# Stage changes of a fused attention and two-layer kernel: operand pool at the bottom, fourth output operand split at once, last product's operands formed in place

## The chip, the cores and the metric

The kernel runs on 1 core of one Trainium2 chip. The metric is the device time of one execution in microseconds (us), as the median of several executions. A profiled execution has a time of its own and a span, which runs from its first to its last instruction. Engines are called PE (matmul), PEld (weight load of the PE), DVE (VectorE), ACT (ScalarE), POOL (GpSimd) and SP (SyncE, whose queue SPq issues the transfers here). L612 means line 612 of the kernel before.

## What is computed

The reference, cut to what matters (all float32; 3072 tokens, width 512):

```
x   = chunked attention with memory keys (4 batches, 8 heads, 768 positions)   # 3072 x 512
h   = x @ w_in;   g = h * tanh(softplus(h));   y = g @ w_out                   # 512 -> 2048 -> 512
yn  = y / sqrt(mean(y*y) + 1e-6) * rms_g
out = (silu(yn @ w_gate) * (yn @ w_val)) @ w_out2                              # 512 -> 1536 -> 512
```

## The kernel before

**Stages.** The core does, one after the other with some overlap: attention (transposes and small matmuls); the first product (w_in) in groups; the output product (w_out) in 48 steps; the gate and value product in groups; and the last product (w_out2) in 12 units. Every float32 operand is split in two float32r parts, a high part written by ACT (L145) and a low part written by DVE (L146), and every product is three matmuls: high by high, high by low, low by high.

**Seven products.** The first, the gate and the last product use a scheme with seven block products instead of eight. An operand block matrix b11, b21, b12, b22 gives seven operands, numbered 1 to 7, some of them sums of blocks. `sum_pieces` forms them: operand 1 is b11; then b11 becomes b12 - b11, a first temporary is b22 - b11, a second is the first minus b21, and b12 becomes b22 - b12; operands 6, 5, 4, 2, 7, 3 are split from the first temporary, b11, the second temporary, b21, b12, b22. `group` multiplies them in the order 1, 6, 5, 4, 2, 7, 3 into four banks X, Y, Z, V: product 2 adds to X (1), 7 to Y (6), 3 to Z (5). Between them ACT copies X to s1 (L622) and Z to z5 (L628), and DVE forms u2 (L625), u3 (L636), and at the end the output blocks (L639, L641), POOL one more (L640).

**Pools in SBUF.** On the left side, above the pools that live through the kernel, lie three pools of the first product in this order from the bottom: `cp` (temporaries, 6 x 1536 bytes a partition, 9216), `gp` (results g on their way out to DRAM, 5 x 3072, 15360) and `tp` (operands, 8 x 6144, 49152). Before the output product they are closed and the same bytes are given, from the bottom, to `gl` (one tile of 4096 bytes), `c` (2 x 2048) and `t` (8 operand tiles of 8192, called T). A late tile waits for the old tiles whose bytes it covers, each until its last reader is done; for a g tile the last reader is its store to DRAM (L110). `gl` and `gr` hold one v tile each; the groups of the gate product take them in turn, and `v_temp` takes them for the two temporaries of `sum_pieces`.

**Output product.** `Feed` loads the g tile of a step from DRAM (L742), applies the activation (ACT L753), and splits it. The first three steps' operands go into borrowed tiles (named s, v, w), the fourth goes into the first T tile, by way of the only sm tile; its split is asked for in `feed.next(1)`, after the first step's matmuls and after that step's share of weight conversion (L194 to L208, then ACT L145 and POOL L146 into w; 16 of them for w_out). A step is 24 matmuls (L725 to L727).

**Last product.** `group3` runs one unit: seven products of 18 matmuls each (six weight tiles, f = 0 to 5, three matmuls each, L854 to L856). `preparing(n)` forms the operands of unit n while the work before it runs, one piece at each step of `group`: those of unit 0 during the last group of the gate product, those of unit n + 1 during unit n. Even units load into raw, raw, sm and s tiles, odd ones into the bytes of weight slot 2 (L835), which the last group of the gate product uses until its last matmul. The sixth weight tile, ("o2", 5), goes in one transfer of 1792 KB into slot 3 (L1176), free when the last group but one is done. A weight tile holds the seven products' parts in the order 1, 2, 4, 3, 5, 6, 7, each 256 KB.

**Order.** The order of the instructions on each engine is fixed when the program is built, by a planner that runs the program on a model of the engines' times and takes what is ready, the earlier in the program first. The engines then run their lists in order. So PE's list mixes products of neighbouring groups where the planner saw a wait.

Of the kernel before, what the change touches and what calls it, by code (L numbers as in the profile page):

```python
# [8 lines left out]
F32 = mybir.dt.float32  # L9
# [4 lines left out]
ALU = mybir.AluOpType  # L14
# [15 lines left out]
def tile_kernel(  # L30
# [15 lines left out]
    nc = tc.nc  # L46
# [23 lines left out]
    wd = {("i", i): nc.dram_tensor(f"wi{i}", (128, SLOT), F32R, kind="Internal").ap()  # L70
          for i in range(F1 // 2)}
# [11 lines left out]
    rawp = ctx.enter_context(tc.tile_pool(name="rawp", bufs=2))  # L83
    cap = ctx.enter_context(tc.tile_pool(name="cap", bufs=3))
    mid_stack = ExitStack()
    cp = mid_stack.enter_context(tc.tile_pool(name="cp", bufs=6))
    gp = mid_stack.enter_context(tc.tile_pool(name="gp", bufs=5))
    tp = mid_stack.enter_context(tc.tile_pool(name="tp", bufs=8))
    late_pools = {}
    psp = ctx.enter_context(tc.tile_pool(name="psp", bufs=1, space=bass.MemoryType.PSUM))  # L90
    bk = [psp.tile([128, 512], F32, name=f"bk{c}") for c in range(6)]
# [11 lines left out]
    def store_later(dst, src):  # L103
        late.append((tick[0] + 2, dst, src))
# [8 lines left out]
    def w_slot(u):  # L113
        pool = w1p if u < NW1 else w2p[0]
        return pool.tile([128, SLOT], F32R, tag=f"w{u}", name="w")
# [3 lines left out]
    def as7(s):  # L119
        return s.rearrange("p (a l f) -> p a l f", a=7, l=2)  # L120

    def w_load(key, u):
        s = w_slot(u)
        nc.sync.dma_start(out=s.bitcast(F32), in_=wd[key].bitcast(F32))
        wtab[key] = as7(s)

    def w_store(key, half):
# [16 lines left out]
    def split(src, hi, lo, eng=None, keep=lambda ins: ins):  # L144
        keep(nc.scalar.copy(hi, src))  # L145
        keep((eng or nc.vector).tensor_tensor(lo, src, hi.bitcast(F32), op=ALU.subtract))  # L146
# [399 lines left out]
    def s_new():  # L546
        return late_pools["s"].tile([128, 2, N2], F32, tag="s", name="s")
# [4 lines left out]
    def c_new():  # L552
        return late_pools["c"].tile([128, N2], F32, tag="c", name="c")
# [4 lines left out]
    def t_pieces(j, x0, x1, new, temp_new, dram, tab):  # L558

        return sum_pieces(j, x0[:, 0:2, :], x0[:, 2:4, :], x1[:, 0:2, :], x1[:, 2:4, :],  # L560
                          new, temp_new, dram, tab)

    def sum_pieces(j, b11, b21, b12, b22, new, temp_new, dram, tab):
        cols = b11.shape[2]
        size = b11.shape[1] * cols
        temp = {}

        def as_block(x):
            return x[:, 0:size].rearrange("p (a n) -> p a n", n=cols)

        def one(p, src):
            t = new()
            if isinstance(t, tuple):
                split(src, *t)
                for l in range(2):
                    store_later(dram[:, p - 1, l].bitcast(F32), t[l].bitcast(F32))
                return
            v = t.rearrange("p l a n -> p l (a n)")[:, :, 0:size]
            v = v.rearrange("p l (a n) -> p l a n", n=cols)
            split(src, v[:, 0], v[:, 1])  # L580
            if dram is not None:
                store_later(dram[:, p - 1].bitcast(F32), t.bitcast(F32))
            tab[j, p] = v

        def sums():
            for p in (2, 4):
                temp[p] = as_block(temp_new(p).rearrange("p a n -> p (a n)"))
            nc.vector.tensor_tensor(b11, b12, b11, op=ALU.subtract)
            nc.vector.tensor_tensor(temp[2], b22, b11, op=ALU.subtract)
            nc.vector.tensor_tensor(temp[4], temp[2], b21, op=ALU.subtract)  # L590
            nc.vector.tensor_tensor(b12, b22, b12, op=ALU.subtract)

        early = [lambda: one(1, b11), sums]
        rest = [lambda: one(6, temp[2]), lambda: one(5, b11), lambda: one(4, temp[4]),
                lambda: one(2, b21), lambda: one(7, b12), lambda: one(3, b22)]
        return early, rest

    def t_load(j, dram, tab):
        for p in ORDER:
            t = t_new2()  # L600
            nc.sync.dma_start(out=t.bitcast(F32), in_=dram[:, p - 1].bitcast(F32))
            tab[j, p] = t
# [10 lines left out]
            nc.tensor.matmul(ps, whi, xl, start=False, stop=False, **more)  # L613
            nc.tensor.matmul(ps, wlo, xh, start=False, stop=kk == 1, **more)  # L614

    def group(mul, banks, n_, c12, c21, c22, temps):

        X, Y, Z, V = banks
        x, y, z, vv = (b_[:, 0:n_] for b_ in banks)
        s1, u2, z5 = temps()  # L620
        mul(1, X, True)
        nc.scalar.copy(s1, x)  # L622
        yield
        mul(6, Y, True)
        nc.vector.tensor_tensor(u2, y, s1, op=ALU.add)  # L625
        yield
        mul(5, Z, True)
        nc.scalar.copy(z5, z)  # L628
        yield
        mul(4, V, True)  # L630
        yield
        mul(2, X, False)
        yield
        mul(7, Y, False)
        u3 = s1
        nc.vector.tensor_tensor(u3, y, s1, op=ALU.add)  # L636
        yield
        mul(3, Z, False)
        nc.vector.tensor_tensor(c12, z, u2, op=ALU.add)  # L639
        nc.gpsimd.tensor_tensor(c22, u3, z5, op=ALU.add)  # L640
        nc.vector.scalar_tensor_tensor(  # L641
            c21, vv, -1.0, u3, op0=ALU.mult, op1=ALU.add
        )
        yield
# [25 lines left out]
    def run(parts, between):  # L670
        while parts:
            for part in list(parts):
                if next(part, "end") == "end":
                    parts.remove(part)
                else:
                    between()
# [3 lines left out]
    def group_banks(of):  # L680
        g = n_group[0]
        n_group[0] += 1
        return [bk[(4 * g + of - 4 + i) % of] for i in range(4)]
# [45 lines left out]
    class Feed:  # L729
# [34 lines left out]
        def next(self, s):  # L764
            self.load(s + 3)
            self.split(s + 3)
            self.load(s + 5)
            return self.out.pop(0)
# [52 lines left out]
    hraw, ttab_h = {}, {}  # L821
# [17 lines left out]
        hraw[n] = parts  # L839

    def h_pieces(n):
        return sum_pieces(n, *hraw.pop(n), t_new2, v_temp, None, ttab_h)

    def group3(n, j, r, between):
        o = s_new()
        o = [o[:, a, :] for a in range(2)]

        def mul(p, bank_, first):
            t = ttab_h[n, p]
            ps = bank_[:, 0:256]  # L850
            more = dict(skip_group_check=not first)
            for f in range(HG):
                w = wtab["o2", f][:, W_AT[p]]
                nc.tensor.matmul(ps, t[:, 0, f], w[:, 0], start=first and f == 0, stop=False, **more)  # L854
                nc.tensor.matmul(ps, t[:, 0, f], w[:, 1], start=False, stop=False, **more)  # L855
                nc.tensor.matmul(ps, t[:, 1, f], w[:, 0], start=False, stop=f == HG - 1, **more)  # L856

        banks = group_banks(8)
        c11 = banks[0][:, 0:256]
        c12, c21, c22 = o[1][:, 0:256], o[0][:, 256:512], o[1][:, 256:512]  # L860
        run([group(mul, banks, 256, c12, c21, c22, lambda: (c_new()[:, 0:256], c12, c22))], between)
        nc.scalar.copy(o[0][:, 0:256], c11)
        for a in range(2):
            row = (2 * j + a) * N2 + 128 * r
            store_later(out[row:row + 128, :], o[a])
# [100 lines left out]
    def reload(pos, seq):  # L966
        if pos < 3:
            w_load(("i", seq[5 + pos]), W_SLOT[seq[5 + pos]])
# [16 lines left out]
    at = {u: 4 * n + 4 for n, u in enumerate(units)}  # L985
# [28 lines left out]
    def late_pool(name, bufs, side="left"):  # L1014
        return ctx.enter_context(tc.tile_pool(name=name, bufs=bufs, side=side, reuse_waits="tile"))
# [5 lines left out]
    for pos, i in enumerate(down[:-1]):  # L1021
        group1(3, i, bt)
        if 1 <= pos <= 3:
            back, u = ((1, 4), (2, 0), (0, 1))[pos - 1]
            w_load(("i", back), u)
# [6 lines left out]
    feed = Feed(steps, g_src, ACTF.Mish)  # L1032
# [15 lines left out]
    late_pools["gl"] = late_pool("gl", 1)  # L1048
    late_pools["c"] = late_pool("c", 2)
    late_pools["t"] = late_pool("t", 8)  # L1050
    pend = []
    sq_new = lambda: [c_new() for _ in range(2)]
    for s, (m, i) in enumerate(steps):
        t = feed.next(s)
# [18 lines left out]
        if m == NB2 - 1 and i in (1, 3, 5, 6):  # L1073
            row_slots.clear()
            f, u = {1: (2, 5), 3: (3, 6), 5: (4, 3), 6: (5, 2)}[i]
# [84 lines left out]
    for jn, j in enumerate(jback):  # L1160
        last = jn == NPAIR2 - 1
        if jn:
            t_load(j, nt_d[j], ttab_n)
            run([group2(j, HG), group2(j, HG + 1)], bt)
            if last:
                w_load(("o2", 1), 1)
                w_load(("o2", 2), 4)
        for f in range(HG + 2 if jn else HG, F2):
            run([group2(j, f)], preparing(0, bt) if last and f == F2 - 1 else bt)
            if last and f == HG + 2:  # L1170
                w_load(("o2", 3), 5)
            elif last and f == HG + 3:
                h_load(0, *units[0])
                w_load(("o2", 4), 6)
            elif last and f == HG + 4:
                w_load(("o2", 5), 3)  # L1176
    h_load(1, *units[1])
    for n, (j, r) in enumerate(units):
        if 0 < n < len(units) - 1:
# [34 lines left out]
```

## Time and profile before

| what | value |
|---|---|
| median of 3 runs | 1191.08 us (1189.69 to 1196.43) |
| the profiled execution's own time | 1190.69 us |
| its span | 1188.9 us |
| PE busy | 1153.8 us, 97% of the span |
| DVE, ACT, POOL busy | 817.5, 621.5, 215.1 us |
| mean granted PE clock | 0.990 |

A busy share near 100% says that PE sets the pace. Time can then be won in PE's few idle stretches and where its granted clock is below 1.00.

### The profile page before, as it was taken

How to read it: one execution, taken by the hardware profiler on the slowest of the kernel's cores; microseconds unless marked ns; L12 is line 12 of the kernel's file. 1: busy time of each engine (PE TensorE's matmuls, PEld its weight loads, DVE VectorE, ACT ScalarE, POOL GpSimd, SP SyncE). 2: the span in 40 equal slices, each digit the busy share in tenths (PEclk: the TensorE clock that was granted, in tenths of full speed). 3: DMA queues.
4: the chain of work that ended last, by engine and by line, in shares of the span. 5: the costliest groups of instructions: out<-in, count | busy, mean ns of one | idle time of the engine just before them, and what ended most of it. 6: DMA issues, size and time to landing. Idle time of an engine off the chain costs nothing.

```text
span 1188.9 us, 22951 instructions
## 1 busy us (share of the span) xinstructions
PE 1153.8 (97%) x9052; PEld 1008.5 (85%) x9052; DVE 817.5 (69%) x1212; ACT 621.5 (52%) x996; POOL 215.1 (18%) x185
## 2 busy tenths in 40 slices
PE   6899899999999899999999999999999999999998
PEld 4789899999999688888878878878888888999998
DVE  4655898854755856675775675976886746887773
ACT  5566566543545866667665443553454423444442
POOL 2010222310132411030131121322221211000000
PEclk8899989999999999999999999999999999999999
DMA  9889869899488764595589388899889878654420
GB/s 188 172 230 217 209 239 264 231 293 300 148 304 289 246 204 129 187 362 163 195 329 393 144 343 333 321 416 391 319 312 377 315 264 293 195 173 142 142 90 36
DMA packets 219132, 294.20 MB, mean 247 GB/s; under 512 B 104208, under 2 KB 168720, under 8 KB 210064
## 3 DMA queue, kind: packets, MB, share of 16 engines
q1 hardware_dynamic: 219024, 292.73, 74.1%
q8 instruction: 71, 1.16, 0.4%
q14 instruction: 37, 0.30, 0.1%
HBM read 181.80 MB, written 110.89 MB: 246 GB/s over the span
## 4 chain that ended last, share of the span: by engine, by line
PE 74%; DMA 8%; DVE 7%; ACT 5%; issue 3%; POOL 2%; SPq 0%; ACTq 0%; POOLq 0%; DVEq 0%
PE bk L612 13%; PE bk L614 12%; PE bk L613 12%; DMA s<-g_scratch 4%; PE bk L856 4%; PE bk L854 4%; PE bk L855 4%; PE bk L726 3%; PE bk L727 3%; PE bk L725 3%; PE bkp L612 2%; PE bkp L614 2%; PE bkp L613 2%; PE bkp L434 2%; PE bkp L483 1%
## 5 line engine op out<-in xcount | busy, mean ns | idle before, releaser
L612 PE MATMUL bk<-T,w 128*128 128x384 f32 (+1 forms) x860 | 317.3, 372 | 5.5 <-ACT g L662 4.1
L613 PE MATMUL bk<-T,w 128*128 128x384 f32 (+1 forms) x860 | 312.5, 363 | 0.0
L614 PE MATMUL bk<-T,w 128*128 128x384 f32 (+1 forms) x860 | 311.6, 364 | 0.0
L612 PEld LDWEIGHTS bk<-T,w 128*128 128x128 f32 x860 | 162.7, 190 | 26.7 <-ACT g L662 4.3
L613 PEld LDWEIGHTS bk<-T,w 128*128 128x128 f32 x860 | 162.5, 189 | 17.3 <-issue 0.2
L614 PEld LDWEIGHTS bk<-T,w 128*128 128x128 f32 x860 | 162.3, 189 | 16.8
L854 PE MATMUL bk<-w,T 128*128 128x256 f32 x396 | 112.3, 284 | 2.9 <-ACT T L145 1.8
L725 PE MATMUL bk<-T,w 128*128 128x512 f32 x276 | 109.1, 396 | 2.9 <-ACT T L145 2.9
L856 PE MATMUL bk<-w,T 128*128 128x256 f32 x396 | 111.4, 282 | 0.2 <-DVE T L146 0.2
L855 PE MATMUL bk<-w,T 128*128 128x256 f32 x396 | 111.4, 281 | 0.0
L726 PE MATMUL bk<-T,w 128*128 128x512 f32 x276 | 109.4, 396 | 0.3 <-DVE T L146 0.3
L727 PE MATMUL bk<-T,w 128*128 128x512 f32 x276 | 108.6, 393 | 0.0
L640 POOL TENSOR_TENSOR v<-c,v 128x512 f32<-128x512 f32 x36 | 51.6, 1436 | 222.3 <-DVE c L636 164.8
L636 DVE TENSOR_TENSOR c<-bk,c 128x512 f32<-128x512 f32 (+2 forms) x72 | 43.1, 599 | 63.4 <-PE bk L614 51.7
L622 ACT COPY c<-bk 128x512 f32<-128x512 f32 (+2 forms) x72 | 37.0, 516 | 83.9 <-PE bk L614 33.3
L146 DVE TENSOR_TENSOR T<-s,T 128x1024 fp32r<-128x1024 f32 (+1 forms) x50 | 61.3, 1235 | 26.0 <-ACT T L145 25.5
L854 PEld LDWEIGHTS bk<-w,T 128*128 128x128 f32 x396 | 75.2, 190 | 4.2 <-ACT T L145 2.9
L855 PEld LDWEIGHTS bk<-w,T 128*128 128x128 f32 x396 | 75.5, 191 | 0.1
L856 PEld LDWEIGHTS bk<-w,T 128*128 128x128 f32 x396 | 75.0, 190 | 0.4 <-DVE T L146 0.4
L753 ACT ACTIVATE s<-s 128x1024 f32<-128x1024 f32 x44 | 46.7, 1061 | 38.6 <-DMA s<-g_scratch 36.6
L725 PEld LDWEIGHTS bk<-T,w 128*128 128x128 f32 x276 | 51.8, 188 | 15.4 <-ACT T L145 3.3
L726 PEld LDWEIGHTS bk<-T,w 128*128 128x128 f32 x276 | 52.0, 188 | 13.2 <-issue 1.2
(218 smaller groups left out, 2309.2 us busy)
## 6 DMA issues: line engine op xcount, KB each, us to landing
T<-nt_scratch SPq DMA_DIRECT2D x35, 1024.0 KB
g_scratch<-g SPq DMA_DIRECT2D x64, 384.0 KB
s<-g_scratch SPq DMA_DIRECT2D x46, 512.0 KB
h_scratch<-s SPq DMA_DIRECT2D x36, 512.0 KB
w<-wg SPq DMA_DIRECT2D x10, 1792.0 KB
wg<-w SPq DMA_DIRECT2D x30, 512.0 KB
raw<-in_moe_w_out_dram SPq DMA_DIRECT2D x28, 512.0 KB
nt_scratch<-T SPq DMA_DIRECT2D x14, 1024.0 KB
```

The source lines that it names most:

```text
L146: keep((eng or nc.vector).tensor_tensor(lo, src, hi.bitcast(F32), op=ALU.subtract))
L612: nc.tensor.matmul(ps, whi, xh, start=first and kk == 0, stop=False, **more)
L613: nc.tensor.matmul(ps, whi, xl, start=False, stop=False, **more)
L614: nc.tensor.matmul(ps, wlo, xh, start=False, stop=kk == 1, **more)
L640: nc.gpsimd.tensor_tensor(c22, u3, z5, op=ALU.add)
L725: nc.tensor.matmul(ps, ahi, bhi, start=start, stop=False)
L726: nc.tensor.matmul(ps, ahi, blo, start=False, stop=False)
L727: nc.tensor.matmul(ps, alo, bhi, start=False, stop=stop)
L753: nc.scalar.activation(x, g, self.act)
L854: nc.tensor.matmul(ps, t[:, 0, f], w[:, 0], start=first and f == 0, stop=False, **more)
L855: nc.tensor.matmul(ps, t[:, 0, f], w[:, 1], start=False, stop=False, **more)
L856: nc.tensor.matmul(ps, t[:, 1, f], w[:, 0], start=False, stop=f == HG - 1, **more)
```

## The change

Four edits. (1) The three pools of the first product change places: operands at the bottom, then g, then the temporaries; the late pools keep their bytes. (2) The fourth output operand is split right where the late pools open, ahead of the first output step in the program. (3) The transfer of ("o2", 5) is cut in three: the part of product 1, those of 2, 4 and 3, those of 5, 6 and 7. (4) The units of the last product form their operands in place: after operand 1, b11 becomes b12 - b11 and b12 becomes b22 - b12; operand 5 is split from b11, then b11 becomes b22 - b11; operand 6 is split from b11, then b11 becomes b11 - b21; then operands 2, 4, 7, 3. The two temporaries in gl and gr are not used there any more, and the units multiply in the order 1, 5, 6, 4, 2, 7, 3. `sum_one` is the inner function `one` of `sum_pieces`, moved out.

```diff
     mid_stack = ExitStack()
+    tp = mid_stack.enter_context(tc.tile_pool(name="tp", bufs=8))
+    gp = mid_stack.enter_context(tc.tile_pool(name="gp", bufs=5))
     cp = mid_stack.enter_context(tc.tile_pool(name="cp", bufs=6))
-    gp = mid_stack.enter_context(tc.tile_pool(name="gp", bufs=5))
-    tp = mid_stack.enter_context(tc.tile_pool(name="tp", bufs=8))
...
-    def w_load(key, u):
+    def w_load(key, u, cuts=()):
         s = w_slot(u)
-        nc.sync.dma_start(out=s.bitcast(F32), in_=wd[key].bitcast(F32))
+        edges = (0,) + cuts + (7,)
+        for a, b in zip(edges, edges[1:]):
+            at = slice(512 * a, 512 * b)
+            nc.sync.dma_start(out=s[:, at].bitcast(F32), in_=wd[key][:, at].bitcast(F32))
...
-        mul(6, Y, True)
-        nc.vector.tensor_tensor(u2, y, s1, op=ALU.add)
-        yield
-        mul(5, Z, True)
-        nc.scalar.copy(z5, z)
-        yield
+        for p in (5, 6) if five_first else (6, 5):
+            if p == 6:
+                mul(6, Y, True)
+                nc.vector.tensor_tensor(u2, y, s1, op=ALU.add)
+            else:
+                mul(5, Z, True)
+                nc.scalar.copy(z5, z)
+            yield
...
     def h_pieces(n):
-        return sum_pieces(n, *hraw.pop(n), t_new2, v_temp, None, ttab_h)
+        b11, b21, b12, b22 = hraw.pop(n)
+        one = lambda p, src: sum_one(n, p, src, t_new2, None, ttab_h)
+        sub = lambda out, a, b: nc.vector.tensor_tensor(out, a, b, op=ALU.subtract)
+        early = [lambda: one(1, b11), lambda: sub(b11, b12, b11), lambda: sub(b12, b22, b12)]
+
+        def p5():
+            one(5, b11)
+            sub(b11, b22, b11)
+
+        def p6():
+            one(6, b11)
+            sub(b11, b11, b21)
+
+        return early, [p5, p6, lambda: one(2, b21), lambda: one(4, b11),
+                       lambda: one(7, b12), lambda: one(3, b22)]
...
     late_pools["t"] = late_pool("t", 8)
+    feed.split(4)
...
-                w_load(("o2", 5), 3)
+                w_load(("o2", 5), 3, (1, 4))
```

## Rows read from the trace of the kernel before

**Rows 1.** Busy time by stretch: length, PE, PEld, DVE, ACT, POOL, PE clock, DMA.

```profile
380.00:401.00 21.00, 17.23 (x73) 13.84 (x72) 16.10 (x23) 14.59 (x22) 7.24 (x7) 0.92 0.72 228
401.00:996.00 595.00, 592.78 (x2573) 482.44 (x2572) 412.02 (x559) 317.31 (x462) 123.31 (x92) 1.00 0.78 290
996.00:1025.00 29.00, 25.98 (x188) 23.77 (x187) 23.77 (x30) 13.92 (x21) 4.15 (x3) 1.00 0.71 227
...
sum 1189.00, PE 1153.76 PEld 1008.55 DVE 817.46 ACT 621.55 POOL 215.11; mean PE 164.82 PEld 144.08 DVE 116.78 ACT 88.79 POOL 30.73
```

**Rows 2.** Who PE waited for: us in total, times, longest us.

```profile
PE bk L725 <- ACT T L145: 2.9, 1, 2.9
...
PE bk L854 <- ACT T L145: 1.8, 3, 1.0
...
PE bk L854 <- DMA w<-wo: 1.0, 1, 1.0
```

**Rows 3.** Timeline of PE around 395 us: start, length, line, operands.

```profile
392.53 0.40 PE L727 MATMUL bkp<-w 128*128 128x512 f32 x1
...
400.81 0.40 PE L725 MATMUL bk<-T,w 128*128 128x512 f32 x1
401.04 0.39 PE L726 MATMUL bk<-T,w 128*128 128x512 f32 x1
```

**Rows 4.** Windows of PE alone: length, busy, instructions, clock, DMA.

```profile
395.80:400.80 5.00, 4.71 (x12) 0.66 0.32 106
```

**Rows 5.** Chain that ended last, 360 to 405 us: start, length, what.

```profile
390.32 4.28 DMA g_scratch<-g
...
394.70 1.05 ACT T L145
```

**Rows 6.** Timelines of ACT, then DVE, before the fourth operand.

```profile
387.74 1.06 ACT L753 ACTIVATE sm<-w 128x1024 f32<-128x1024 f32 x1 [0.19 <-DVE w L146]
...
390.61 1.67 DVE L202 SCALAR_TENSOR_TENSOR ca<-raw,ca 128x512 int32<-128x512 int32 x1
...
395.78 1.23 DVE L146 TENSOR_TENSOR T<-sm,T 128x1024 fp32r<-128x1024 f32 x1 [2.67 <-ACT T L145]
```

**Rows 7.** Timeline of POOL: the last of the 16 conversions of w_out.

```profile
414.49 1.56 POOL L146 TENSOR_TENSOR w<-ca,w 128x512 fp32r<-128x512 f32 x1 [2.11 <-ACT w L145]
```

**Rows 8.** Timeline of PE around 1000 us.

```profile
1000.69 0.40 PE L614 MATMUL bk<-T,w 128*128 128x512 f32 x1
...
1003.59 0.28 PE L854 MATMUL bkp<-w,T 128*128 128x256 f32 x1
```

**Rows 9.** Timelines of DVE and of ACT around 1000 us.

```profile
998.53 1.22 DVE L720 TENSOR_TENSOR s<-s,v 128x1024 f32<-128x1024 f32 x1
999.79 0.96 DVE L589 TENSOR_TENSOR v<-s,raw 128x768 f32<-128x768 f32 x1
...
1004.34 0.95 DVE L146 TENSOR_TENSOR T<-v,T 128x768 fp32r<-128x768 f32 x1
...
1005.93 0.59 ACT L628 COPY v<-bk 128x512 f32<-128x512 f32 x1
```

**Rows 10.** Chain that ended last, 985 to 1025 us.

```profile
996.13 6.96 DMA w<-wo
...
1010.77 4.23 DMA w<-h_scratch
```

**Rows 11.** Timeline of PE around 1021 us.

```profile
1019.52 0.28 PE L855 MATMUL bk<-w,T 128*128 128x256 f32 x1
1019.64 0.28 PE L856 MATMUL bk<-w,T 128*128 128x256 f32 x1
...
1023.13 0.28 PE L854 MATMUL bk<-w,T 128*128 128x256 f32 x1
```

**Rows 12.** Timeline of ACT: unit 2's operand 6, and X of unit 2.

```profile
1030.35 0.84 ACT L145 CAST T<-v 128x768 fp32r<-128x768 f32 x1 [2.94 <-DVE v L589]
...
1037.54 0.38 ACT L622 COPY c<-bk 128x256 f32<-128x256 f32 x1 [1.32 <-PE bk L856]
```

More of the change, by code (lines that the diff above doesn't have):

```diff
@@ L561, in t_pieces, with sum_one @@
                           new, temp_new, dram, tab)
+    def sum_one(j, p, src, new, dram, tab):
+        cols = src.shape[2]
+        size = src.shape[1] * cols
+        t = new()
+        if isinstance(t, tuple):
+            split(src, *t)
+            for l in range(2):
+                store_later(dram[:, p - 1, l].bitcast(F32), t[l].bitcast(F32))
+            return
+        v = t.rearrange("p l a n -> p l (a n)")[:, :, 0:size]
+        v = v.rearrange("p l (a n) -> p l a n", n=cols)
+        split(src, v[:, 0], v[:, 1])
+        if dram is not None:
+            store_later(dram[:, p - 1].bitcast(F32), t.bitcast(F32))
+        tab[j, p] = v
     def sum_pieces(j, b11, b21, b12, b22, new, temp_new, dram, tab):
@@ L569, in as_block @@
             return x[:, 0:size].rearrange("p (a n) -> p a n", n=cols)
[L571 to L583, printed above, removed]
+        one = lambda p, src: sum_one(j, p, src, new, dram, tab)
         def sums():
@@ L614, in product, with group @@
             nc.tensor.matmul(ps, wlo, xh, start=False, stop=kk == 1, **more)
-    def group(mul, banks, n_, c12, c21, c22, temps):
+    def group(mul, banks, n_, c12, c21, c22, temps, five_first=False):
         X, Y, Z, V = banks
@@ L860, in group3 @@
         c12, c21, c22 = o[1][:, 0:256], o[0][:, 256:512], o[1][:, 256:512]
-        run([group(mul, banks, 256, c12, c21, c22, lambda: (c_new()[:, 0:256], c12, c22))], between)
+        run([group(mul, banks, 256, c12, c21, c22, lambda: (c_new()[:, 0:256], c12, c22),
+                   True)], between)
         nc.scalar.copy(o[0][:, 0:256], c11)
```

## The prediction, on record before the changed kernel ran

> **What bounds the kernel now.** I read the windows by stage first. PE is busy for 1153.8 of 1189 us, and from 401 to 996 us it misses 2.2 of 595 us, so there nothing but matmuls is on the path. Two later places, which are the ones that the diff touches, are not full: 3.8 us idle between 380 and 401 us, at a mean clock of 0.92, and 3.0 us idle between 996 and 1025 us [rows 1]. Then the list of what PE waited for: the high part of a T tile once for 2.9 us (L725), and in the last product high parts three times, 1.8 us together, and the sixth weight tile for 1.0 us [rows 2]. Last the timelines, to price each place by the starts of matmuls, since a wait can also cost clock or hold up the next wait.
>
> *Place A, the fourth output operand.* A step's matmul takes 0.23 us from start to start (400.81 to 401.04). Behind the one at 392.53 came 12 matmuls before the one at 400.81 [rows 3, 4]; at full rate that one starts at 392.53 + 13 x 0.23 = 395.5. The loss is 400.8 - 395.5 = 5.3 us. Only 2.9 of it is the wait; behind it the granted clock of the 5 us with the 12 matmuls was 0.66, so for most of them the lower of the two levels, 1.2 GHz, after an idle stretch of about 3 us [rows 4]. What was late: the sm tile was ready at 387.74 + 1.06 = 388.8 [rows 6], but ACT's cast to T started at 394.70, when the store of the last g tile had landed, 4.28 us after its issue at 390.32 [rows 5]. In the old layout the first T tile lies on bytes 8192 to 16384 of the region, and gp holds 9216 to 24576: it covers three g tiles.
>
> *Place B, unit 0 of the last product.* After 1000.69 a matmul of the old group ends its slot at 1000.92; five matmuls of the unit start before the one at 1003.59 [rows 8]. At 0.12 us each [rows 11] that one was due at 1000.92 + 5 x 0.12 = 1001.5. Loss 2.1 us. What was late: the temporary for operand 6 was formed at 999.79, right behind the end (998.53 + 1.22 = 999.75) of the product that frees its v tile [rows 9]; and the weight tile landed at 996.13 + 6.96 = 1003.1 [rows 10].
>
> *Place C, unit 1.* After 1019.64 seven matmuls start before the one at 1023.13, due at 1019.64 + 8 x 0.12 = 1020.6 [rows 11]. Loss 2.5 us. What was late begins at B: the second temporary held the other v tile until its low part was done at 1004.34 + 0.95 = 1005.3, so the old group's z5 copy into that tile came at 1005.93 [rows 9], its product 3 after that, and only then, at 1010.77, the load of unit 1 into weight slot 2, whose first part took 4.23 us [rows 10].
>
> **The change part by part.** The sum starts from the profiled execution's 1190.69 us, 0.4 below the median of the runs.
>
> *Pools and early split (A).* With tp at the bottom (bytes 0 to 49152) the first T tile covers parts of the second and third operand tile of the first product, whose last readers are matmuls of the last group, over by about 392.8 - 24 x 0.23 = 387.3, since the third output step alone lies behind them [rows 3]. I take it that this late pool hands out its lowest tile first, as it seems to now: the wait for the g store fits that tile. Then the cast starts at 388.8 and ends at 389.9 (1.05 us, [rows 5]), and the low part (1.23 us, [rows 6]) ends between 391.1 and, behind the conversion that held DVE from 390.61 to 392.3, 393.5 [rows 6]. PE wants the high part at 392.53 + 0.23 = 392.8 and, with three high matmuls first, the low one at 393.4. Without an idle stretch there is no reason left for the low clock. So 5.3 us are removed, less 0 to 0.5 for the low part; I take 5.2. No instruction is added by the early split; it moves one activation, cast and subtraction (1.06, 1.05 and 1.23 us) ahead of conversions on ACT and DVE. Late next are the conversions: the last ends at 414.49 + 1.56 = 416.1 [rows 7]. It is the second half of the eighth step's weights. If the fourth step begins at 392.8 and a step is 24 x 0.23 = 5.5 us, the eighth begins at 392.8 + 4 x 5.5 = 414.8 and wants that half at 417.6. The cover is 1.5 us; pushed back by one cast, 1.05, it still holds. Without cover the price is at most those 1.05 us. The later T tiles now lie on g and temporaries; they wait to about 394.6 (390.32 + 4.28) for the g store, and steps six and seven want them at 392.8 + 2 x 5.5 = 403.8 and later.
>
> *In place (B and C).* Operation counts do not change: a unit has seven splits and four subtractions before and after, 0.95 us each on DVE. What goes is the use of gl and gr by units. Unit 0's operands 5 and 6 then wait for their blocks, which L589 found loaded, and for T tiles freed by the old group's products 1 and 6; nothing waits for 998.53. A subtraction in place now also waits for ACT's cast of the same block; behind it in DVE's list stand the running unit's u2 and u3 (L625, L636), and for u2 waits PE's product 7, with products 4 and 2, 4.3 us, as cover. The old group's z5 has its v tile as soon as the group two before is done with it, its products 7 and 3 run without the detour, and slot 2 is free at about 1000.9 + 6 x 0.23 = 1002.3 at the latest. Unit 1's load then starts some 8 us earlier than 1010.77, with unit 0's 126 matmuls, 15 us, to cover it. So place C loses its 2.5 us; I take all of it.
>
> *The weight tile in three (B).* Two more issues on SP; the nearest row is the whole tile's 6.96 us for 1792 KB [rows 10]. If the pieces share the way evenly they all land at about 1003.1, as now; if in order, the first 256 KB lands well before 1001. Product 1's last three matmuls want it near 1001, product 5's want the third piece at 1000.9 + 18 x 0.12 = 1003.1, or 1004.5 with the old group's product 3 first. So between 0 and 2.1 us of place B come back; I take 1.6, nearer the upper end, because PE has the old group's last products and operand 6's matmuls as other work.
>
> The Trainium skill speaks against this edit: "DMA: Bandwidth & Descriptors", Bandwidth and Rules for kernel authors, wants at least 1 MiB per transfer, and "SBUF — State Buffer", The DMA setup-cost knee, puts a fixed cost of about 2 us on each transfer. No run here shows yet what a piece costs; if the two added fixed costs fell one after another on the last piece, an estimate from that page is 4 us, and the sum would be 1190.7 - 5.2 - 2.5 - 1.6 + 4 = 1185.4 instead of the one below.
>
> *Order of products 5 and 6.* Same matmuls, other banks first. Product 7 needs u2 and product 3 needs z5; both still have at least two products (2 x 2.2 us) between. Taken at 0; without that cover it costs one 0.4 us copy a unit.
>
> Sum: 1190.7 - 5.2 - 2.5 - 1.6 = 1181.4 us, -0.8%.
>
> **The rivals.**
>
> *The pieces come late.* The nearest row for a transfer with others behind it is the 4.23 us of a unit load's first part, 384 KB of four [rows 10]. One after another, three such end 12.7 us after 996.1, at 1008.8, 4.3 us behind the 1004.5 at which product 5 wants its piece. Then B costs up to 4.3 where it costs 2.1 now: 1190.7 - 5.2 - 2.5 + 2.2 = 1185.2. What the skill's page says of transfers under 1 MiB would work in this way. Against it: 1792 KB landed in 6.96 us whole [rows 10], so the way is not that slow. Chance 0.12.
>
> *Place A stays, in another form.* If the first T tile is one that now lies on g (the sixth to eighth of the eight), the same store releases it, and the 5.3 us stay: 1190.7 - 2.5 - 1.6 = 1186.6. Or the conversions become late. For it: which tile is taken is the planner's choice. Chance 0.12.
>
> *The planner gives it back.* Orders of all engines behind 380 us are laid anew; if new stalls eat the gains, the change does not do what it says: about 1190. Against it: 2.2 us idle in 595 us [rows 1] show that the order has slack nearly everywhere. Chance 0.07.
>
> *Slower: the in-place chain binds in each unit.* Operand 6 now waits for operand 5's cast (0.84), low part (0.95) and a subtraction (0.95), and needs its own cast (0.84), 3.6 us in all, while product 5 lasts 2.2. If units were formed only as PE reaches them, each of 11 units would lose 1.4 us, 15 us: 1190.7 - 5.2 + 15 = 1200. It decides from a lead of less than 1.4 us between forming operand 6 and its product. Unit 2 had its operand 6 cast at 1030.35, while its X was copied only at 1037.54 [rows 12]: a lead of 7 us. Chance 0.06.
>
> **How the numbers follow.** Forecast 0.63, and the rivals 0.12, 0.12, 0.07 and 0.06. The likeliest is 1181.4. Below it only the full 9.9 us of the three places and what new order might add: 1178.5. Above it the two rivals that leave one place open: 1187. Within 0.5% means above 1185.1 here, about what a measurement can tell from no change. The forecast is faster but for its worst end, and half of the first rival joins it: faster 0.69; the rest of the two middle rivals and the lost gain, same 0.24; slower 0.07.
>
> **What would show it.** Right: no PE wait on L725 by L145 near 393 us and a granted clock of 1.00 from 392 to 400 us; no wait of the unit matmuls for T in the first two units; the load of unit 1 issued near 1002 less the shift of about 5 us from A; the third weight piece landed within 8 us of the first's issue. Wrong: a new PE wait of over 1 us for a w piece, for POOL's w or DVE's T in the fourth to eighth step, or a PE wait that repeats in each unit of the last product.

## The result, and the profile after

The changed kernel takes 1180.46 us (1178.21 to 1183.48), against 1190.67 us (1188.47 to 1196.43) for the kernel before beside it: a ratio of 0.991, interval 0.988 to 0.993, so 0.9% faster. Its profiled execution took 1181.62 us, with a span of 1179.8 us. In the changed file the lines have moved: L725 to L727 are now L734 to L736, L854 to L856 are L877 to L879, L145 and L146 are L148 and L149, L628 is L637, and L853 is the subtraction in place.

Windows after (length, PE, PEld, DVE, ACT, POOL, PE clock, DMA); the first is the stretch of [rows 1], the second the one that held place A:

```profile
380.00:401.00 21.00, 20.35 (x96) 17.12 (x96) 16.98 (x24) 14.56 (x21) 7.39 (x5) 1.00 0.78 258
393.00:401.00 8.00, 8.00 (x37) 6.56 (x36) 7.63 (x9) 5.34 (x8) 2.01 (x1) 1.00 0.71 219
401.00:660.00 259.00, 258.68 (x1118) 209.70 (x1117) 172.97 (x217) 177.08 (x216) 52.78 (x34) 1.00 0.70 253
...
991.00:1020.00 29.00, 28.65 (x223) 27.68 (x222) 21.39 (x28) 11.58 (x18) 3.32 (x3) 1.00 0.74 226
```

The second stretch in the kernel before:

```profile
393.00:401.00 8.00, 4.91 (x13) 3.61 (x14) 5.30 (x8) 6.92 (x10) 1.39 (x2) 0.79 0.46 140
```

Place A is closed: PE is busy for all 8 us behind 393 at a clock of 1.00 and does 37 matmuls, where it did 13 at 0.79 before. Where unit 0 and unit 1 of the last product begin, 0.35 us of 29 are idle, against 3.0 of 29 before [rows 1]. Between 960 and 1030 us PE's waits are down to one line. The kernel before had three there: the two lines on L854 in [rows 2], and 0.2 us on L856 for a low part.

```profile
PE bkp L877 <- DMA w<-wo: 0.4, 1, 0.4
```

Timelines after: PE at the first, fourth and later output steps, with the two RMS matmuls that serve as marks below (L810); then ACT and DVE before the fourth operand:

```profile
386.68 0.63 PE L734 MATMUL bk<-w 128*128 128x512 f32 x2
...
392.50 0.40 PE L736 MATMUL bkp<-w 128*128 128x512 f32 x1
392.73 0.63 PE L734 MATMUL bk<-T,w 128*128 128x512 f32 x2
...
431.21 1.02 PE L810 MATMUL bkp<-c,ones 128*128 128x512 f32 x2
...
655.53 1.02 PE L810 MATMUL bk<-w,ones 128*128 128x512 f32 x2
...
387.70 1.06 ACT L762 ACTIVATE sm<-w 128x1024 f32<-128x1024 f32 x1 [0.19 <-DVE w L149]
...
389.94 1.04 ACT L148 CAST T<-sm 128x1024 fp32r<-128x1024 f32 x1
```

The cast to T starts at 389.94, not at 394.70 [rows 5], and waits for nothing that the profile names. PE takes the tile at 392.73, one matmul pitch behind the step before. The low part follows on DVE from 391.01 for 1.58 us, and PE first reads it at 393.43. The last conversion of w_out starts at 410.86, where it started at 414.49 [rows 7].

Timelines after around 1000 us: ACT (the old group's z5 copy), SP (the weight pieces, then the loads of the units) and PE:

```profile
985.52 0.58 ACT L637 COPY v<-bk 128x512 f32<-128x512 f32 x1
...
990.90 1.27 SPq L127 DMA_DIRECT2D w<-wo  x3
...
996.89 7.50 SPq L844 DMA_DIRECT2D w<-h_scratch  x4
...
1000.43 0.39 PE L877 MATMUL bkp<-w,T 128*128 128x256 f32 x1 [0.35 <-DMA w<-wo]
```

Against [rows 9, 10], the z5 copy comes 20.4 us earlier (985.52 for 1005.93) and unit 1's load 13.9 us earlier (996.89 for 1010.77), of which only some 5 us are the shift from place A.

**Three marks, three stretches.** Whole times here spread by 4 us and more, and part of that is made before the change begins: the first matmul pair of the output product started between 384.3 and 390.2 us in the fourteen profiled executions of this study. So each kernel is also read by stretches: A from that pair (386.73 before, 386.68 after) to the first RMS matmul; M on to the last RMS matmul; L from there to the span's end. Timeline of PE before, the same marks:

```profile
386.73 0.63 PE L725 MATMUL bk<-w 128*128 128x512 f32 x2
...
436.50 1.02 PE L801 MATMUL bkp<-c,ones 128*128 128x512 f32 x2
...
660.88 1.02 PE L801 MATMUL bk<-w,ones 128*128 128x512 f32 x2
```

| kernel | A | M | L | median us | ratio, interval |
|---|---|---|---|---|---|
| before | 49.8 | 224.4 | 528.0 | 1190.67 | |
| after | 44.5 | 224.3 | 524.3 | 1180.46 | 0.991 [0.988, 0.993] |
| e1_pools | 49.0 | 224.3 | 529.4 | 1189.70 | 0.999 [0.998, 1.001] |
| e2_split | 47.3 | 223.9 | 527.9 | 1190.33 | 1.001 [0.999, 1.002] |
| e3_t_lowest | 44.6 | 225.2 | 529.3 | 1185.77 | 0.996 [0.995, 0.998] |
| e4_warm | 47.7 | 224.3 | 527.9 | 1187.88 | 0.999 [0.998, 1.000] |
| e5_cut | 49.0 | 225.4 | 529.8 | 1191.54 | 1.000 [0.999, 1.002] |
| e6_whole | 44.5 | 224.7 | 524.3 | 1182.11 | 0.992 [0.990, 0.994] |
| e7_inplace | 49.0 | 224.4 | 523.4 | 1184.89 | 0.995 [0.993, 0.996] |
| e8_pieces | 44.6 | 225.1 | 523.8 | 1182.36 | 0.993 [0.991, 0.995] |
| e9_temp_gr | 44.5 | 226.0 | 523.6 | 1183.14 | 0.993 [0.991, 0.995] |
| e10_temp_gl | 44.6 | 224.0 | 523.7 | 1180.55 | 0.991 [0.989, 0.993] |
| e11_two_temps | 44.6 | 225.1 | 527.1 | 1183.09 | 0.993 [0.991, 0.996] |
| e12_six_first | 44.5 | 224.5 | 525.0 | 1181.21 | 0.991 [0.989, 0.993] |

The stretches are of one profiled execution each. A takes two groups of values, 44.5 to 44.6 and 47.3 to 49.8; L takes 523.4 to 525.0, and 527.1 to 529.8. M varies by 2 us without regard to the edits. Ratios are against runs of the kernel before on the same chip, whose medians were 1189.99, 1190.63, 1191.01 and 1192.51 in the four groups of runs.

### The profile page after: what moved, and what is told of

Same layout as the page of the kernel before. It is cut to its first block, busy times and chain, and to the rows that moved or that the text cites. A ratio compares the mean times of both kernels' runs of the same rounds, so it can differ in the third digit from the quotient of the medians.

```text
span 1179.8 us, 22946 instructions
## 1 busy us (share of the span) xinstructions
PE 1149.5 (97%) x9052; PEld 1007.3 (85%) x9052; DVE 816.4 (69%) x1212; ACT 620.3 (53%) x996; POOL 213.7 (18%) x185
## 4 chain that ended last, share of the span: by engine, by line
PE 77%; DMA 7%; DVE 7%; ACT 5%; issue 2%; POOL 1%; SPq 1%; ACTq 0%; POOLq 0%; DVEq 0%
PE bk L619 14%; PE bk L621 13%; PE bk L620 13%; PE bk L877 4%; PE bk L879 4%; PE bk L878 4%; DMA s<-g_scratch 3%; PE bk L735 3%; PE bk L736 3%; PE bk L734 3%; PE bkp L619 2%; PE bkp L620 2%; PE bkp L621 2%; PE bkp L437 2%; PE bkp L486 1%
## 5 line engine op out<-in xcount | busy, mean ns | idle before, releaser
L877 PE MATMUL bk<-w,T 128*128 128x256 f32 x396 | 111.7, 283 | 0.0
L879 PE MATMUL bk<-w,T 128*128 128x256 f32 x396 | 111.6, 282 | 0.0
L734 PE MATMUL bk<-T,w 128*128 128x512 f32 x276 | 109.0, 396 | 0.0
L736 PE MATMUL bk<-T,w 128*128 128x512 f32 x276 | 107.9, 392 | 0.0
L645 DVE TENSOR_TENSOR c<-bk,c 128x512 f32<-128x512 f32 (+2 forms) x72 | 43.1, 598 | 59.8 <-PE bk L621 47.3
L149 DVE TENSOR_TENSOR T<-s,T 128x1024 fp32r<-128x1024 f32 (+1 forms) x50 | 60.0, 1210 | 29.3 <-ACT T L148 28.8
L877 PEld LDWEIGHTS bk<-w,T 128*128 128x128 f32 x396 | 75.2, 190 | 0.1
L879 PEld LDWEIGHTS bk<-w,T 128*128 128x128 f32 x396 | 75.2, 190 | 0.0
L734 PEld LDWEIGHTS bk<-T,w 128*128 128x128 f32 x276 | 51.8, 188 | 12.1 <-issue 0.7
```

The costliest lines, as they stand in the source:

```text
L734: nc.tensor.matmul(ps, ahi, bhi, start=start, stop=False)
L736: nc.tensor.matmul(ps, alo, bhi, start=False, stop=stop)
```

## Experiments

**Place A: the tile, the early split, or both.** The two edits one at a time on the kernel before; then both in another way, with the old pool order but T as the lowest of the late pools, so that the first T tile lies on the temporaries:

```diff
# e1_pools: the first hunk of the change alone (tp, gp, cp in place of cp, gp, tp)
# e2_split: the early split alone
+    feed.split(4)
# e3_t_lowest: the late pools opened as t, c, gl (not gl, c, t), and
+    feed.split(4)
```

> The kernel before with the new order of the pools alone; each engine's list of instructions is that of before, so only waits differ. Theory (the T tile waited for the g store): the cast to T no longer waits for the store, but it still stands in ACT's list behind a weight cast that ended at 393.7 us before. It starts about 1 us earlier, at 393.7 instead of 394.7, and PE's wait for it falls from 2.9 to about 1.9 us; total 1187 to 1190 against 1190.7. Rival (the tile alone decides): the wait goes and the time is 1185.4. Rival (the place in the program alone decides): the wait stays at 2.9 us.

> The kernel before with the early split alone. Theory: the cast stands earlier in ACT's list but still waits for the g store that lands near 394.6 us, so it starts no earlier; PE waits 2.9 us, the clock behind it is about 0.66 for 5 us, total 1190.7. Rival (the place in the program decides): no wait, 1185.4.

> The kernel before with the old order of the early pools, but the T tiles lowest among the late ones, so that the first T tile lies on the temporaries c instead of on g, and with the early split. Theory (what counts is which old tile lies under the first T tile): POOL reads the last c until 390.3 us, the cast follows at once, no wait of PE over 0.5 us, granted clock 1.00 from 393 to 401 us, total 1185.4 as with operands at the bottom. Rival (only operands at the bottom free the tile in time): 1190.7.

Neither edit alone changes the time; both together do, even with the pools of the first product in their old order. ACT's timelines say why, first e1_pools:

```profile
391.64 0.62 ACT L145 CAST w<-ca 128x512 fp32r<-128x512 f32 x1 [1.84 <-DVE ca L208]
392.16 1.04 ACT L145 CAST T<-sm 128x1024 fp32r<-128x1024 f32 x1
```

then e2_split:

```profile
393.72 1.04 ACT L145 CAST T<-sm 128x1024 fp32r<-128x1024 f32 x1 [3.64 <-DMA g_scratch<-g]
```

and e3_t_lowest:

```profile
388.89 1.05 ACT L145 CAST T<-sm 128x1024 fp32r<-128x1024 f32 x1 [0.26 <-POOL g L640]
```

In e1_pools the store no longer holds the cast; the cast of converted weights ahead of it in ACT's list does, 1.84 us behind DVE. The chain shows that the last store of g lands only at 388.85 + 4.35 = 393.20, 1.0 us behind the start of the cast:

```profile
388.85 4.35 DMA g_scratch<-g
```

PE's wait of 1.8 us alone would not show it: e5_cut and e7_inplace, with the old pools and without the early split, wait 1.8 us too, since there the cast follows that weight cast at once. So how much the store costs in the old layout differs between executions. In e2_split the cast stands first, but the store of g releases it, and all of ACT's list waits 3.64 us with it; PE's wait was 1.9 us at a clock of 1.00, both less than was expected, and A is 47.3. Only where the tile is free and the cast stands early does A shrink to 44.6. Which bytes the tile covers is not the point, only that they are not g's.

**The clock behind the wait.** To see whether the low clock comes from the idle stretch, 13 matmuls that nothing reads, 3.0 us at the pitch of 0.23, are put ahead of the fourth step in the kernel before:

```diff
+        if s == 2:
+            whi = wtab["o1", 2 * i][0]
+            for r in range(13):
+                nc.tensor.matmul(banks1(1)[r % KC], whi[:, 0:128], t[0][:, 0, :])
```

> The kernel before with 13 more matmuls of 0.23 us behind the third output step, into banks that the next pass writes anew, so that PE works through the 2.9 us of its wait. Theory (the low clock comes from the idle stretch): the cast stays at 394.7 us, PE idles under 0.5 us, the 12 matmuls behind come at 0.23 instead of 0.42 us, granted clock 1.00; the work is more and the time is less, by about 2.2 us: 1188.5. Rival (the slow matmuls come from something else, as operands just written): clock 0.66 stays, total 1190.7 or more.

The planner put seven of them into the first step, so that all that follows comes later, and six into the wait itself. PE's timeline in e4_warm, each lot in one row, and windows of the stretch behind it:

```profile
385.13 1.80 PE L1059 MATMUL bk<-w 128*128 128x512 f32 x7
...
391.67 1.56 PE L1059 MATMUL bk<-w 128*128 128x512 f32 x6
393.07 0.65 PE L725 MATMUL bk<-T,w 128*128 128x512 f32 x2
...
393.00:395.70 2.70, 2.40 (x10) 1.71 (x10) 2.67 (x4) 2.70 (x4) 0.00 (x0) 1.00 0.03 14
395.70:401.00 5.30, 5.30 (x24) 4.32 (x24) 5.30 (x7) 3.96 (x7) 2.34 (x1) 1.00 0.77 245
```

A is 47.7: the full 44.6 and the 3.0 of the filler. The operand is nearly as late as before (its cast starts 7.5 us behind the first pair, 8.0 before), but the clock stays at 1.00, and 2.1 us of the 5.2 are back; the time is 0.14% lower (interval 0.04 to 0.25%). So place A was 2.9 us of wait and some 2 of clock, as the prediction split it.

**The last product: weight pieces.** The cut alone on the kernel before, the changed kernel without the cut, and the changed kernel with the third piece (products 5, 6, 7) sent second:

```diff
# e5_cut, on the kernel before          # e6_whole, on the changed kernel
-  w_load(("o2", 5), 3)                 -  w_load(("o2", 5), 3, (1, 4))
+  w_load(("o2", 5), 3, (1, 4))         +  w_load(("o2", 5), 3)
# e8_pieces, on the changed kernel
+        parts = list(zip(edges, edges[1:]))
-        for a, b in zip(edges, edges[1:]):
+        for a, b in parts[:1] + parts[:0:-1]:
```

> The kernel before with the sixth weight tile's transfer cut in three, alone. Theory: PE's 1.0 us wait for the tile shrinks to 0 to 0.5 us, since product 1's part comes first; the waits for T of units 0 and 1 and the whole 5.3 us of the fourth output operand stay: 1189.5 to 1190.7. Rival (pieces cost): the last piece lands later than 6.96 us behind the issue and PE waits as long as before or longer: 1190.7 to 1193.

> The changed kernel with that transfer whole again. Theory (the cut is worth little): the tile lands about 7 us behind its issue, near 998 us; the wait of 0.35 us for the third piece goes and one for product 1's part may come, 0 to 1 us; total 1180 to 1181.5. Rival (the cut is needed): PE waits 1 us or more for the tile, 1181.5 to 1183.

> The changed kernel with the three pieces in the order in which the products want them: 1, then 5, 6, 7, then 2, 4, 3. Theory: the piece with product 5 lands some 2 us earlier, and the remaining wait of 0.35 us for it near 1000 us goes with nothing in its place: 0.3 to 0.6 us less, not to be told from 1180.5. Rival (the pieces share the way and land together): the wait stays.

The cut is worth nothing that these runs can tell, with or without the rest. PE's waits in e5_cut between 975 and 1030 us:

```profile
PE bk L857 <- ACT T L148: 1.7, 4, 1.0
PE bk L859 <- DVE T L149: 0.9, 2, 0.7
PE bkp L857 <- ACT T L148: 0.2, 1, 0.2
```

The 1.0 us wait for the weight tile [rows 2] is gone, and the waits for T tiles grew from 2.0 to 2.8: the operands were as late as the weights. Its L of 529.8 is no sign of a price of the cut, since the clock fell to 0.83 between 1020 and 1030 us, behind a wait for T in unit 1. e6_whole's 1182.1 us lies in the range of the rival that the cut is needed, but its one PE wait in the last product is 0.3 us and its L is that of after. The chain in the changed kernel has the third piece, issued last of the three,

```profile
991.75 8.64 DMA w<-wo
```

and in e6_whole the uncut tile:

```profile
992.07 9.40 DMA w<-wo
```

So from the first issue the tile took 9.5 us in pieces (990.90 to 1000.39) and 9.40 whole, where it had taken 6.96 in the kernel before [rows 10]. What is new in both is that the unit loads are issued while it is under way. Without them the pieces cost nothing: in e5_cut, by the semaphore updates in its trace (the marks that a finished transfer sets), the last one landed 6.98 us behind the first issue (997.10 to 1004.08). In e11_two_temps below, where one unit load was issued meanwhile, it took 7.4 us (989.66 to 997.05):

```profile
990.51 6.54 DMA w<-wo
```

That the loads make the difference is the likely reading and not shown: e7_inplace, with a whole tile and the same loads beside it, took 7.8 us (994.22 to 1002.01, by the same updates). In e8_pieces, where no PE wait is left in the last product, L is 0.5 us shorter than after; its time doesn't show that.

**The last product: in place, or the order of 5 and 6.** The fourth edit alone on the kernel before; the changed kernel with one temporary put back, in gr for operand 4 or in gl for operand 6; with both put back, product 5 still first; and in place, but product 6 multiplied first:

```diff
# e9_temp_gr: after operand 6 is split
-            sub(b11, b11, b21)
+            sub(b4[0], b11, b21)          # b4: a v tile in gr or gl, split as operand 4
# e10_temp_gl: after operand 5 is split
-            sub(b11, b22, b11)
+            sub(b6[0], b22, b11)          # b6: a v tile, split as operand 6
# e11_two_temps: h_pieces
+        early, rest = sum_pieces(n, *hraw.pop(n), t_new2, v_temp, None, ttab_h)
+        return early, [rest[1], rest[0], *rest[2:]]
# e12_six_first: group3's call of group
-    run([group(mul, banks, 256, c12, c21, c22, lambda: (c_new()[:, 0:256], c12, c22),
-               True)], between)
+    run([group(mul, banks, 256, c12, c21, c22, lambda: (c_new()[:, 0:256], c12, c22))], between)
```

> The kernel before with the operands formed in place and product 5 first, alone. Theory: the waits of unit matmuls for T in units 0 and 1 go, unit 1's load is issued some 9 us earlier in its stage, and at most 1 us of wait for the whole weight tile stays: 3.5 to 4.6 us less, 1186 to 1187; the 2.9 us wait near 393 us and the low clock behind it stay. Rival (the gain near 1000 us comes from the cut): 1189 to 1190.7.

> The changed kernel, but operand 4's block is formed in the gr tile instead of in place. Theory (place C came from the v tile held by a temporary): the old group's z5 copy waits for operand 4's low part again, unit 1's load is issued some 5 to 9 us later, and PE waits 1 to 2.5 us in unit 1: 1182 to 1183. Rival (C came from the order of the operands or from a longer chain on DVE): no such wait, 1180.5.

> The changed kernel, but operand 6's block is formed in the gl tile instead of in place. Theory (the release of the v tile made operand 6 late): its subtraction waits again for the end of the last but one gate group's product, so operand 6 comes 2 to 4 us later than in the changed kernel; with product 5 multiplied first PE has 2.2 us of other work, so it waits 0 to 2 us in unit 0 and not at all in unit 1: 1180.5 to 1182.5. Rival (operand 6 is not late for that reason): no change of any wait, 1180.5.

> The changed kernel, but each unit of the last product forms its operands through both temporaries in the gl and gr tiles, as before; product 5 still stands ahead of product 6. Theory (what places B and C cost came from the two temporaries): they come back. The stretch from the second RMS matmul (655.53 us in the changed kernel) to the span's end, 524.3 us there and 528.0 in the kernel before, goes to 527.5 to 529.5, the PE waits for T tiles in the last product are there again, and the time is 1184 to 1186. Rival (the order of products 5 and 6 brought it): the stretch stays at 523.5 to 524.5 and the time at 1180 to 1182.5.

> The changed kernel, operands still formed in place and in the same order, but the units multiply product 6 ahead of product 5, as before. Theory (in place is enough, the order is worth nothing but cover for operand 6): the stretch from the second RMS matmul to the span's end stays at 523.5 to 525.0 us, with at most 1 us of new PE waits for operand 6 in unit 0, and the time at 1180 to 1183. Rival (operand 6, formed last of the two, is late for every unit): about 1.4 us in several of the 12 units, the stretch at 527 or more, the time at 1184 or more.

e7_inplace has no PE wait at all between 960 and 1030 us and an L of 523.4, with A at its old 49.0: the fourth edit does all of B and C by itself. Its L is 4.6 us shorter than the 528.0 of the kernel before, which is the 2.1 and 2.5 us that the two places were priced at; its time, 1184.9, is below the range expected. With both temporaries back (e11_two_temps) 2.8 of the 3.7 us of L come back; L and the time, 1183.1, both lie between the two ranges expected and don't decide by themselves. Its PE waits in the last product, two of the three matmuls that waited, its z5 copy and its load of unit 1:

```profile
PE bk L864 <- ACT T L148: 1.0, 1, 1.0
PE bk L866 <- DVE T L149: 0.8, 2, 0.5
...
1010.72 0.39 PE L866 MATMUL bk<-w,T 128*128 128x256 f32 x1 [0.49 <-DVE T L149]
1014.14 0.39 PE L864 MATMUL bk<-w,T 128*128 128x256 f32 x1 [1.01 <-ACT T L148]
...
999.45 0.59 ACT L637 COPY v<-bk 128x512 f32<-128x512 f32 x1
...
1004.50 3.29 SPq L844 DMA_DIRECT2D w<-h_scratch  x4
```

The copy and the load are late together again. Counted from the last RMS matmul they come at 345.2 and 350.2 us, as in the kernel before (345.1 and 349.9), and at 330.0 and 341.4 in the changed kernel. That is place C: the three waits lie between 1010.7 and 1015.0, where unit 1 begins. Place B does not come back with the temporaries: in unit 0 PE waits for no operand that the profile names, with product 5 first and the tile in pieces. With product 6 first but in place (e12_six_first) unit 0 has no wait for an operand either; L is 525.0 and the one new cost is a wait of 0.9 us for the weight tile. So either half of the fourth edit is enough for unit 0's operands, and beside operands formed in place the order is worth about half a microsecond.

e9_temp_gr was meant to bring place C back alone, and didn't. Its z5 copy, its load of unit 1 and its operand 4:

```profile
991.78 0.58 ACT L637 COPY v<-bk 128x512 f32<-128x512 f32 x1
...
1002.05 4.00 SPq L844 DMA_DIRECT2D w<-h_scratch  x4
...
1006.50 0.83 ACT L148 CAST T<-v 128x768 fp32r<-128x768 f32 x1 [0.69 <-DVE v L853]
```

A temporary that is asked for only after operand 6 comes behind the z5 copy, not ahead of it, so the group's end was never held; L is 523.6 with no PE wait, so its time, 1183.1, though just above the range expected for such waits, is no sign of them. e10_temp_gl, a first temporary alone, is as harmless (523.7). There the subtraction does wait for the last but one group's product again, and comes 11.0 us later than in the changed kernel, counted from the last RMS matmul; expected were 2 to 4 us, and PE waited for nothing:

```profile
996.48 0.95 DVE L853 TENSOR_TENSOR v<-s,raw 128x768 f32<-128x768 f32 x1
```

What held up the old group is the two temporaries as `sum_pieces` forms them, both early and the second out of the first. Whether the second alone would do it if it were formed early, no run shows.

## Why the prediction was right

**Place A, 5.2 predicted.** A went from 49.8 to 44.5, so 5.2 in this pair; against the 49.0 of e1_pools, e5_cut and e7_inplace it is 4.4, since their wait was 1.8 and not 2.9 us. So the 5.2 is the size in this pair of executions, at the upper end. Both halves hold: the wait by e3_t_lowest, the clock by e4_warm. The assumption that the late pool hands out its lowest tile first is borne out by the rows of e2_split and e3_t_lowest. That the early split is needed beside the new tile was only implied in the prediction; e1_pools shows it. The cast came 1.1 us later than worked out (389.94, not 388.8), behind a weight cast that still stood ahead of it, and PE had cover for that. The gain was kept: the first and the last RMS matmul both come 5.3 us earlier; the conversions, named as late next, moved forward with the rest.

**Place C, 2.5, and place B, 1.6: 4.1 together.** L went from 528.0 to 524.3, so 3.7. The mechanism told for C (temporaries hold a v tile, z5 late, slot 2 late, load late) is shown by e11_two_temps and e7_inplace for the two temporaries formed together and early. The prediction put it on the second alone; e9_temp_gr, which formed that one later, had no such wait. The load of unit 1 came at 996.89, as the sign for it said (1002 less about 5).

**The weight pieces: mis-sized and misplaced.** The prediction gave them the say over B, 0 to 2.1 us back, 1.6 taken. They bring nothing that shows (e5_cut, e6_whole); B came back by the fourth edit (e7_inplace); for unit 0's operands either half of it, the forming in place or the order of 5 and 6, was enough (e12_six_first, e11_two_temps). That a term of 1.6 held is luck as far as its reason goes: another edit paid it. The last piece landed 9.5 us after the first issue, not within 8: the row of 6.96 us was of a tile that no unit load was issued beside, and the same change moved the unit loads there. What the lateness cost is the 0.4 us wait at 1000.43; the four runs in place without any wait have an L of 523.4 to 523.8, 0.5 to 0.9 us shorter.

**The rule against the cut.** The prediction set beside it an estimate of 4 us for two added fixed costs, from the Trainium skill, "SBUF — State Buffer", The DMA setup-cost knee. Here three pieces took 6.98 us where the whole tile took 6.96 (e5_cut and the kernel before), and 9.5 where it took 9.40 (after and e6_whole), so no such cost shows when they are issued one behind the other; the trace does not bear the estimate out.

**The rivals.** Pieces that come late happened, at 0.4 us and not at 4.3. Place A in another form did not. The planner gave nothing back: M is 224.4 and 224.3. The in-place chain doesn't bind: from 1030 to 1176 us PE is busy for all 146 us before and after, in this order:

```profile
1030.00:1176.00 146.00, 146.00 (x1227) 146.00 (x1226) 114.56 (x148) 65.05 (x98) 11.58 (x10) 1.00 0.44 131
1030.00:1176.00 146.00, 146.00 (x1226) 146.00 (x1226) 109.74 (x141) 60.58 (x94) 10.26 (x10) 1.00 0.40 119
```

**Sum.** 5.2 of A and 3.7 of L are 8.9 of the 9.1 us between the two spans (1188.9 and 1179.8), the rest being M, the start and rounding, against 9.3 predicted; 1181.4 was forecast, and 1181.62 is the profiled execution, 1180.46 the median. The parts alone add up too: e3_t_lowest 0.4% and e7_inplace 0.5% make the 0.9% of the whole.

## What to carry to other kernels

A late operand has two conditions, the bytes that it waits for and its place in the list of the engine that forms it; change both or expect nothing. Price a stall by matmul starts, since the idle stretch can cost nearly as much again in clock. A transfer's time from a quiet stretch was only a lower bound here, since the same change moved other loads beside it, and a temporary cost nothing here by existing, only by standing ahead of something that needed its tile. A sum can come true with a term paid by another edit than the one it was given to; only runs of the single edits tell.

## What the runs showed of the hardware

The clock's fall is not settled by the length of the one idle stretch. In e1_pools PE idled 1.8 us and then 0.5, and ran at the lower level (1.2 GHz) soon after; in e2_split it idled 1.9 and then 0.3, and stayed at 1.00. Windows of both, first e1_pools:

```profile
394.00:396.00 2.00, 1.47 (x5) 0.98 (x5) 1.97 (x4) 2.00 (x3) 0.00 (x0) 0.75 0.01 4
396.00:398.00 2.00, 2.00 (x6) 1.63 (x5) 2.00 (x3) 2.00 (x4) 0.00 (x0) 0.50 0.58 197
```

then e2_split:

```profile
394.00:396.00 2.00, 0.96 (x3) 0.49 (x3) 1.20 (x2) 2.00 (x4) 0.00 (x0) 1.00 0.00 0
396.00:398.00 2.00, 1.92 (x8) 1.60 (x9) 1.97 (x4) 2.00 (x3) 0.00 (x0) 1.00 0.00 0
```

The same goes for place B: with idle stretches of 0.6 and 1.0 to 1.1 us the kernel before, e2_split and e4_warm kept the clock there, and L was 527.9 to 528.0; e1_pools and e3_t_lowest, with 0.6 and 1.3 to 1.5 us, ran some microseconds at the lower level (0.64 from 1002 to 1004 us in e1_pools, 0.50 from 1000 to 1002 in e3_t_lowest) and L was 529.3 to 529.4. Where unit 1 begins, the kernel before idled 0.2, 1.0 and 0.2 us and stayed at 1.00; e5_cut idled as long, with one more stretch of 0.2 ahead, and had 0.83 from 1020 to 1030 us. What decides it isn't shown by these runs. It is worth about 1.4 us in e1_pools and e3_t_lowest; whether it makes part of the spread between runs of one kernel isn't shown either.
